# A seventh-product form for one more sequence unit, and two more gate/up units prepared inside the first FFN quarter

## The chip, the cores and the metric

The kernel runs on one core of a Trainium2 chip. The metric is the device time of one execution in microseconds, the median of three runs. Beside it stands one profiled execution with its trace.

The core has engines with queues of their own: TensorE (PE, with its weight loads as PEld), VectorE (DVE), ScalarE (ACT), GpSimd (POOL) and SyncE (SP). Each works through its own instructions in program order, so an instruction that waits holds back all that stands behind it on its engine. SP issues nearly all the DMAs.

## The reference

```python
a = einsum("bsd,ed->bse", x, dft_hid_re);  b = einsum("bsd,ed->bse", x, dft_hid_im)   # x after layer norm
y = einsum("ts,bse->bte", dft_seq_re, a) - einsum("ts,bse->bte", dft_seq_im, b)
h = A_x + y
gate, up = layernorm(h) @ w_gate, layernorm(h) @ w_up
out = h + (gelu(gate) * up) @ w_down
```

The sequence has 2048 rows, the model 448 features, the feed-forward part 1792. All is float32 outside; inside, each operand is split into a high and a low float16 part, and a product is three matmul terms (high by high, low by high, high by low).

## The kernel before

**DFT stage (0 to 347.7 us).** 16 row tiles of x are normalised and multiplied with the hidden DFT (feature tiles, matmuls at L457). The sequence DFT has 8 passes over the output rows; in each, 8 sequence units `u` (two row tiles each) are summed in PSUM (matmuls at L574). A unit is "plain" or an "S" unit. A plain unit is 24 matmuls of 448 columns. An S unit (listed in `S_UNITS`, 3 to 7 here) multiplies blocks as seven products of sums of blocks instead of eight, the Strassen scheme, in 42 matmuls of 224 columns. It pays for that with sums: in each pass VectorE forms `wsum` from the raw transform block `wr` (L518, L520, L522), ScalarE its high part and VectorE its low part (`wss`), and both form high and low of the raw blocks that are used alone (`ws`). The two feature tiles of an S unit need sums of `b` once.

**The planner.** A function `arranged()` gets every DFT piece of work as a task with an engine, a cost, a due time (shifted by kind through the table `SHIFT`) and what must come before it. It simulates the engines and writes the instructions in the order that it finds. Gate/up weights are prepared there too: raw weights are loaded, four sums are formed, high and low parts are made piece by piece (`gu_p`) and stored to DRAM (`w_dram`), from where a finished unit is loaded later as one tile `gw`.

**FFN stage (347.7 us to the end).** It has four quarters of 256 rows. In each, 14 gate/up units run one after the other; `t` counts them, 0 to 55. A unit has three PSUM banks X, Y, Z and seven products (matmuls at L1199, weights from `gw`); ScalarE does the gelu, VectorE and GpSimd the combinations into `hh`. In quarter 0 (t = 0 to 13) TensorE does nothing else; from t = 14 on, 21 matmuls of the down projection (`acc_d`, L1144) are woven into each unit. The down weights `wd` come in seven chunks: loaded (L230), summed on GpSimd, split by ScalarE and VectorE in a 448-column and a 1120-column part.

The order of TensorE in quarter 0 is written out by hand. At unit t: `x_close(t)` 5 matmuls, `x_open(t+1)` 6, `y_mid(t)` 6, `z_open(t+1)` 6, `y_open(t+1)` 6, `y_close(t)` 5, `z_close(t)` 5. So unit t+1 starts while unit t is being finished.

**Late units.** The units in `LATE` are not prepared in the DFT stage but in quarter 0, by `Weights.beat(k)` (L683), two beats to a unit: beat 2t stands after `y_mid(t)`, beat 2t+1 at the end of unit t. `late_prep` (L1421) starts unit f at beat `LATE[f]` and runs k = 0 to 5: sums in k = 0 and 1, one high part in each of k = 1 to 4, one low part in each of k = 2 to 5. The four parts are two of the raw weights (512 and 256 columns, from `gu_raw`) and two of the sums (512 each, from `gu_s`). The finished tile is stored at unit f for the later quarters (L698). Before the change, units 4, 8 and 12 are late.

## Time and profile before

| | |
|---|---|
| median of three runs | 706.2 us (705.64 to 706.41) |
| profiled execution, span of all instructions | 703.5 us |
| TensorE busy | 697.0 us |
| VectorE busy | 563.2 us |
| ScalarE busy | 408.0 us |
| GpSimd busy | 198.8 us |
| DMA moved | 139.74 MB |

The profiled execution's own time is given by its span, from the first to the last instruction; the median of the runs is 2.7 us above it. In the lines of a profile a number after a line label is the engine, the operation, what it writes and reads by the names of the program, the shape and the count; then the busy time and the mean of one in ns, then the idle time just before. In a timeline the first number is the start from the beginning of the span, the second the duration.

### The profile page before, as it was taken

What the parts mean: (1) busy time and instruction counts of PE and PEld (TensorE: products, weight loads), DVE (VectorE), ACT (ScalarE), POOL (GpSimd) and SP (SyncE); (2) the same over time, 40 slices, a digit from 0 to 9 for tenths busy, and PEclk for the clock granted to TensorE, in tenths of its full rate; (3) what the DMA queues carried; (4) which work ended last, traced back from release to release, by engine and by line L of the source; (5) the groups of instructions that cost most, each with busy time, mean ns of one, the idle gap of its engine ahead of it and who ended that gap; (6) DMA issues with size and microseconds to landing.
All of it is one profiled execution on the core that took longest, in us unless ns stands there. A gap on an engine that the chain in (4) does not pass through costs nothing.

```text
span 703.5 us, 15378 instructions
## 1 busy us (share of the span) xinstructions
PE 697.0 (99%) x6046; PEld 584.1 (83%) x6046; DVE 563.2 (80%) x1170; ACT 408.0 (58%) x862; POOL 198.8 (28%) x225
## 2 busy tenths in 40 slices
PE   8999999999999999999999999999999999999998
PEld 5556578878787878778888889999999999999998
DVE  6999999999999897989578877575765755786786
ACT  5776674667576565656267765555555544455432
POOL 0000000000000000001136754474664745647342
PEclk9999999999999999999999999999999999999999
DMA  9554555687988867777579665658466594545401
GB/s 330 160 128 114 142 170 184 233 245 227 228 275 202 283 177 261 262 253 281 182 258 353 204 211 170 191 180 199 170 195 190 178 200 173 181 158 166 151 27 54
DMA packets 81849, 139.74 MB, mean 199 GB/s; under 512 B 41712, under 2 KB 59376, under 8 KB 81776
## 3 DMA queue, kind: packets, MB, share of 16 engines
q1 hardware_dynamic: 81776, 138.76, 63.5%
q8 instruction: 47, 0.77, 0.5%
q14 instruction: 26, 0.21, 0.1%
HBM read 109.25 MB, written 20.19 MB: 184 GB/s over the span
## 4 chain that ended last, share of the span: by engine, by line
PE 95%; DMA 1%; ACT 1%; DVE 1%; issue 1%; SPq 0%; ACTq 0%; DVEq 0%
PE acc L574 38%; PE acc_d L1144 15%; PE pY L1199 14%; PE pZ L1199 9%; PE pX L1199 9%; PE ab L457 9%; DMA x<-in_x_dram 1%; DVE dn_w L110 0%; ACT dn_w L106 0%; SPq L429 0%; ACT xn_h L254 0%; DVE st_x L354 0%; DVE hh L1209 0%; ACT wd L106 0%; ACT g L1252 0%
## 5 line engine op out<-in xcount | busy, mean ns | idle before, releaser
L1199 PEld LDWEIGHTS <-gw 128*128 128x128 f16 x2184 | 213.1, 98 | 23.7 <-issue 1.0
L574 PE MATMUL acc<-b,ws 128*128 128x224 f16 (+1 forms) x1296 | 204.6, 301 | 0.0
L574 PEld LDWEIGHTS <-ws 128*128 128x128 f16 x1296 | 125.6, 98 | 53.2
L1199 PE MATMUL pY<-hops,gw 128*128 128x256 f16 x952 | 129.1, 273 | 0.0
L1144 PE MATMUL acc_d<-wd,dn_w 128*128 128x224 f16 x1050 | 122.3, 259 | 0.0
L574 PE MATMUL acc<-b,wss 128*128 128x224 f16 x960 | 118.2, 259 | 0.0
L235 POOL TENSOR_TENSOR wd_s<-wd 128x448 f32<-128x448 f32 x7 | 10.1, 1442 | 346.8 <-DMA wr<-in_w_seq_dram 330.0
L1144 PEld LDWEIGHTS <-dn_w 128*128 128x128 f16 x1050 | 101.1, 98 | 2.9
L574 PEld LDWEIGHTS <-wss 128*128 128x128 f16 x960 | 92.3, 98 | 0.1
L106 ACT ACTIVATE ws<-wr 128x256 f16<-128x256 f32 (+2 forms) x104 | 62.4, 637 | 41.1 <-PE acc L574 16.1
L1199 PE MATMUL pZ<-hops,gw 128*128 128x256 f16 x616 | 85.5, 273 | 0.4 <-DVE hh L1209 0.3
L1276 POOL TENSOR_TENSOR hh<-hh,c 128x256 f32<-128x256 f32 x56 | 46.3, 828 | 139.7 <-ACT c L1274 139.5
L1199 PE MATMUL pX<-hops,gw 128*128 128x256 f16 x616 | 83.3, 273 | 0.0
L112 DVE SCALAR_TENSOR_TENSOR ws<-wr,ws 128x256 f16<-128x256 f32 (+2 forms) x104 | 70.6, 709 | 1.4 <-ACT ws L106 1.3
L110 DVE TENSOR_TENSOR dn_w<-hh,dn_w 128x256 f16<-128x256 f32 x50 | 25.3, 506 | 53.1 <-ACT dn_w L106 52.8
L106 ACT ACTIVATE wss<-wsum 128x1024 f16<-128x1024 f32 x40 | 42.1, 1053 | 36.8 <-DVE wsum L522 21.1
L457 PEld LDWEIGHTS <-xT 128*128 128x128 f16 x352 | 33.9, 98 | 32.8 <-ACT xT L420 1.5
L110 DVE TENSOR_TENSOR dn_w<-dn_s,dn_w 128x640 f16<-128x640 f32 x50 | 54.6, 1092 | 7.4 <-ACT dn_w L106 6.7
L1243 ACT ACTIVATE u<-pY 128x256 f32<-128x256 f32 x56 | 21.4, 382 | 61.4 <-PE pY L1199 61.3
L1291 POOL TENSOR_TENSOR dn_s<-hh 128x256 f32<-128x256 f32 x42 | 52.8, 1258 | 0.0
L112 DVE SCALAR_TENSOR_TENSOR wss<-wsum,wss 128x1024 f16<-128x1024 f32 x40 | 48.8, 1220 | 4.1 <-ACT wss L106 4.0
L1238 ACT ACTIVATE pY<-pX 128x256 f32<-128x256 f32 x56 | 20.6, 368 | 50.3 <-PE pX L1199 50.3
...
## 6 DMA issues: line engine op xcount, KB each, us to landing
...
```

The source lines that it names most:

```text
L106: A.activation(dst, src, AF.Copy, scale=scale)
L110: V.tensor_sub(dst, src, hi)
L112: V.scalar_tensor_tensor(dst, src, scale, hi, op0=ALU.mult, op1=ALU.subtract)
L235: G.tensor_sub(s[:, 2:4], t[:, 0:2], t[:, 2:4])
L457: PE.matmul(feat[i][r][:, :D], xT[i][:, kx, :], w[:, kw, r * D : (r + 1) * D], start=n == 0, stop=n == 10,)
L574: PE.matmul(banks[k][:, cols], lhs, rhs, start=k not in begun, stop=stop, skip_group_check=True)
L1144: PE.matmul(acc[k // 2][:, k % 2 * HD : (k % 2 + 1) * HD], a_of(la, a), b_of(lb, b), start=first and m == 0 and k % 2 == 0, stop=last and ...
L1199: PE.matmul(ps, w[:, wl, wa + ws, :], ops[:, m + ms, :], start=first and n == 0, stop=last and n == len(terms) - 1, skip_group_check=True,)
L1238: A.activation(self.Y, self.X, AF.Copy)
L1243: A.activation(self.u2, self.Y, AF.Copy, scale=SC)
L1276: G.tensor_mul(c22, c22, self.c12)
L1291: E.tensor_sub(s[:, 2:4], t[:, 1:4:2], t[:, 0:4:2])
```

## The change

- Unit 2 becomes an S unit: `S_UNITS` is (2, 3, 4, 5, 6, 7). The raw parts of every S unit are made in one instruction of 768 columns where there were two of 256 and 512.
- In the DFT stage the statistics of the x tiles of units 7 and 4 go from VectorE to ScalarE, and two small steps of the reciprocal square roots too. The sums, splits and transposes of one normalised block of h (block (1,1), pass 3) go from the DFT stage to t = 0 to 4 of the FFN.
- `LATE` is {4: 1, 6: 6, 9: 11, 11: 16, 13: 21}: five late units instead of three, in five beats each instead of six. There are two raw buffers, and the next late unit's raw load is issued at k = 0 of the one before. The store is issued one beat after the last.
- Down's chunks are loaded from t = 4 on and prepared at t = 6 to 19; before they stood at t = 0 to 15. The preparation of the h blocks (2,0), (2,1) is spread differently over t = 14 to 27.
- The tables `SHIFT` and `HOLD` of the planner have other numbers, and the order of units in a pass is another.

```diff
-    S_UNITS, ... = (3, 4, 5, 6, 7), 3, 3, 2, 2
+    S_UNITS, ... = (2, 3, 4, 5, 6, 7), 3, 3, 2, 2
+    BY_SCALAR = (7, 4)
...
         if is_s(u):
-            return [(w[0], slice(0, 1), r[:, 0:1]), (w[0], slice(1, 3), r[:, 2:4])]
+            return [(w[0], slice(0, 3), r[:, 1:4])]
...
-            self.raw = pool.tile([P, 2, 6, P], F32, tag="raw", name=f"gu_raw{f}")
+            self.raw = pool.tile([P, 2, 6, P], F32, tag="raw", bufs=bufs, name=f"gu_raw{f}")
...
         def beat(self, k):
...
-            if k > 1:
-                s0, s1, src = parts[k - 2]
+            for n in ((), (), (0, 1), (2,), (3,))[k]:
+                s0, s1, src = parts[n]
                 lo_part(self.slots(1, s0, s1, src), src, self.slots(0, s0, s1, src), W_SC)
-            if 0 < k < 5:
-                s0, s1, src = parts[k - 1]
+            for n in ((), (0, 1), (2,), (3,), ())[k]:
+                s0, s1, src = parts[n]
                 hi_part(self.slots(0, s0, s1, src), src, W_SC)
...
-    LATE = {4: 0, 8: 7, 12: 15}
+    LATE = {4: 1, 6: 6, 9: 11, 11: 16, 13: 21}
...
+    WD0 = 6
+
+    def down_mid(t):
+        n, odd = divmod(t - WD0, 2)
+        if odd and 0 <= n < NC:
+            down_hi(n, 1)
+            if n + 1 < NC:
+                down_load(n + 1)
+        elif 0 < n < NC:
+            down_sums(n)
...
     def late_prep(beat):
-        if beat not in late_beats:
-            return
-        f, k = late_beats[beat]
-        gu[f].beat(k)
-        after = [v for v in LATE if v > f]
-        if k == 3 and after:
-            gu_late(after[0])
-        if k == 5:
-            gw[f] = gu[f].w
+        for f, k in late_beats.pop(beat, ()):
+            gu[f].beat(k)
+            after = [v for v in LATE if v > f]
+            if k == 0 and after:
+                gu_late(after[0])
+            if k == 1:
+                gw[f] = gu[f].w
+            if k == 4:
+                at(late_stores, beat + 1, f)
+        for f in late_stores.pop(beat, ()):
+            gu[f].store()
...
             cur.y_mid()
             late_prep(2 * t)
-            if t in LATE:
-                gu[t].store()
-            if t > 0 and t % 2 == 0 and t < 2 * NC:
-                down_hi(t // 2 - 1, 1)
+            do(t, 1)
+            down_mid(t)
             nxt.z_open()
             nxt.y_open()
             cur.y_close()
             cur.z_close()
             dn_ahead(t)
-            if t > 0:
-                down_prep(t - 1)
+            do(t, 2)
+            down_prep(t - WD0)
             late_prep(2 * t + 1)
+            do(t, 4)
```

Three places in the order of the instructions carry the numbers of the prediction.

The first is VectorE around the last late unit. Before, unit 12 was the last, and its low parts (`gw12` written from `gu_raw12` and `gu_s12`) stood among the work of units 8 to 10:

```order
L1209 SCALAR_TENSOR_TENSOR c12_8_5179<-pZ_8_5087,u2_8_5100 128x256
L112 SCALAR_TENSOR_TENSOR wd_4572<-wd_s_3_5054,wd_4572 128x1120
L112 SCALAR_TENSOR_TENSOR gw12_5149<-gu_raw12_4957,gw12_5149 128x512
L1209 SCALAR_TENSOR_TENSOR hh0_4599<-pZ_9_5153,u3_9_5216 128x256
L112 SCALAR_TENSOR_TENSOR gw12_5149<-gu_raw12_4957,gw12_5149 128x256
L1266 SCALAR_TENSOR_TENSOR hh0_4599<-pY_9_5134,g1_9_5197 128x256
L1209 SCALAR_TENSOR_TENSOR c12_9_5247<-pZ_9_5153,u2_9_5166 128x256
L112 SCALAR_TENSOR_TENSOR wd_4572<-wd32_4_5052,wd_4572 128x448
L112 SCALAR_TENSOR_TENSOR gw12_5149<-gu_s12_5117,gw12_5149 128x512
```

Now unit 13 is the last; its low parts stand among the work of units 11 and 12 (c12_11 is the last combination of unit 11, hh0 from pZ_12 follows the middle of unit 12, the pieces of `dn_w` are operands of the down projection):

```order
L1264 SCALAR_TENSOR_TENSOR c12_11_5458<-pZ_11_5359,u2_11_5372 128x256
L1347 TENSOR_TENSOR dn_s1_5460<-hh0_4652 128x128
L114 SCALAR_TENSOR_TENSOR wd_4625<-wd_s_2_5355,wd_4625 128x1120
L114 SCALAR_TENSOR_TENSOR gw13_5426<-gu_raw13_5218,gw13_5426 128x512
L114 SCALAR_TENSOR_TENSOR gw13_5426<-gu_raw13_5218,gw13_5426 128x256
L1264 SCALAR_TENSOR_TENSOR hh0_4652<-pZ_12_5432,u3_12_5494 128x256
L114 SCALAR_TENSOR_TENSOR gw13_5426<-gu_s13_5393,gw13_5426 128x512
L1321 SCALAR_TENSOR_TENSOR hh0_4652<-pY_12_5411,g1_12_5475 128x256
L1264 SCALAR_TENSOR_TENSOR c12_12_5529<-pZ_12_5432,u2_12_5445 128x256
L112 TENSOR_TENSOR dn_w0_5531<-hh0_4652,dn_w0_5531 128x256
L112 TENSOR_TENSOR dn_w0_5531<-dn_s0_5387,dn_w0_5531 128x640
L114 SCALAR_TENSOR_TENSOR wd_4625<-wd32_3_5430,wd_4625 128x448
```

Behind the last of these rows stands the fourth low part of `gw13`. On TensorE unit 13 opens (X) inside unit 12, with these rows; the third weight load is the first that reads a low part:

```order
L1254 MATMUL pX_12_5404<-hops0_167,gw12_5186 128x256
L1254 LDWEIGHTS gw13_5426 [waits Activation_49]
L1254 MATMUL pX_13_5477<-hops0_167,gw13_5426 128x256
L1254 LDWEIGHTS gw13_5426
L1254 MATMUL pX_13_5477<-hops0_167,gw13_5426 128x256
L1254 LDWEIGHTS gw13_5426 [waits DVE_49]
```

So the distance between the last late unit's low parts and their first use went from two units to less than one.

The second place is the last down chunk (6), on VectorE. Before, its 1120-column low part stood in unit 15, five units ahead of its first use at t = 20:

```order
L1266 SCALAR_TENSOR_TENSOR hh1_5516<-pY_15_5574,g1_15_5617 128x256
L1209 SCALAR_TENSOR_TENSOR c12_15_5684<-pZ_15_5619,u2_15_5603 128x256
L112 SCALAR_TENSOR_TENSOR wd_4572<-wd_s_6_5449,wd_4572 128x1120
```

Now it stands at the end of unit 19 (and its high part on ScalarE behind u2_20):

```order
L1321 SCALAR_TENSOR_TENSOR hh1_5605<-pY_19_6038,g1_19_6079 128x256
L1264 SCALAR_TENSOR_TENSOR c12_19_6144<-pZ_19_6081,u2_19_6062 128x256
L114 SCALAR_TENSOR_TENSOR wd_4625<-wd_s_6_6064,wd_4625 128x1120
L282 TENSOR_TENSOR tt_2_0_6159<-xn_h2_0_5667 128x256
```

It moved by four units, to just ahead of the matmuls of t = 20 that read it.

The third place is the store of the last late unit. SP's queue now has it here, between the loads of units 15 and 16 and that of chunk 4:

```order
L734 DMA w_dram11_164<-gw11_5258 128x3584
L247 DMA wd32_3_5430<-in_w_down_dram 128x896
L1121 DMA gw15_5468<-w_dram1_154 128x3584
L1121 DMA gw16_5539<-w_dram2_155 128x3584
L734 DMA w_dram13_166<-gw13_5426 128x3584
L247 DMA wd32_4_5570<-in_w_down_dram 128x896
```

On VectorE the first write of quarter 1's `hh1` (its pool takes over the space of `gw13` and the raw weights) stands behind these rows, and it waits for a DMA:

```order
L112 TENSOR_TENSOR dn_w1_5616<-hh0_4652,dn_w1_5616 128x256 [waits Activation_49]
L112 TENSOR_TENSOR dn_w1_5616<-dn_s1_5460,dn_w1_5616 128x640 [waits DVE_49,Activation_49]
L1264 SCALAR_TENSOR_TENSOR hh1_5605<-pZ_14_5572,u3_14_5639 128x256 [waits DMAHW5_49,DMAHW3_49,DMAHW6_49,DVE_49,Activation_49]
L1347 TENSOR_TENSOR dn_s2_5642<-hh0_4652 128x128
```

The semaphore DMAHW5 is the one that the store of `gw13` signals; before, the last late store was that of `gw12`, two units earlier.

More of the change, by code (lines that the diff above doesn't have):

```diff
@@ L128, in act_moments, with half_of @@
         A.activation(junk, src, AF.Square, bias=mv[:, 0:1], accum_out=mv[:, 1:2])
+    def half_of(mv, tag, pool=small, of=1):
+        n = mv.shape[1]
+        r = pool.tile([P, 4, n], F32, tag=f"r{n}" if pool is small else f"r_{tag}", name=f"r_{tag}")
+        A.activation(r[:, 1], mv[:, :, 1], AF.Identity, scale=-0.5 / (of * X_SC**2), bias=half_eps)
+        return r
     def root(mv, tag, of=1):
@@ L328 @@
     xt, xs, xT, norm_x = {}, {}, {}, {}
+    by_scalar = tuple((2 * u, 2 * u + 1) for u in BY_SCALAR)
+    junk = p1.tile([P, D], F16, name="junk")
     x_pairs = x.rearrange("(u g p) d -> u p g d", g=2, p=P)
@@ L356, in x_stats, with x_moments, x_of @@
             V.bn_aggr(mv[:, g, :], st)
+    def x_moments(i, tiles):
+        if i == tiles[0]:
+            norm_x[tiles] = small.tile([P, 2, 2], F32, tag="mv2", name=f"mv_x{i}")
+        act_moments(norm_x[tiles][:, tiles.index(i), :], xt[i][0], junk)
+    def x_of(tiles):
+        return D if tiles in by_scalar else 1
     def x_root(*tiles):
-        norm_x[tiles] = norm_x[tiles], root(norm_x[tiles], f"x{tiles[0]}")
+        mv, of, tag = norm_x[tiles], x_of(tiles), f"x{tiles[0]}"
+        r = half_of(mv, tag, small, of) if of > 1 else None
+        norm_x[tiles] = mv, root(mv, tag, of), r
     def x_rstd_steps(*tiles):
-        mv, sd = norm_x.pop(tiles)
+        mv, sd, r = norm_x.pop(tiles)
         found = []
-        steps = rstd_steps(found, mv, sd, f"x{tiles[0]}")
+        steps = rstd_steps(found, mv, sd, f"x{tiles[0]}", of=x_of(tiles), r=r)
         next(steps)
@@ L703 @@
     for k, u in enumerate(ORDER):
-        slots += [("F", i) for i in tiles_of[k]]
-        due = [v for v in ready if not is_s(v) or ORDER.index(v) < k - 1]
-        if k:
-            slots += [("U", 0, v) for v in due[:1]]
-            ready = [v for v in ready if v not in due[:1]]
+        for i in tiles_of[k]:
+            slots.append(("F", i))
+            if i % 2 == HALF.get(k, 1):
+                due = [v for v in ready if ORDER.index(v) < k - (2 if is_s(v) else BEHIND)]
+                slots += [("U", 0, v) for v in due[:1]]
+                ready = [v for v in ready if v not in due[:1]]
         ready.append(u)
@@ L714 @@
     mixed = plain[:]
-    for n, s in zip((1, 3, 4, 5, 7), S_UNITS):
+    for n, s in zip((1, 2, 3, 5, 6, 7), S_UNITS):
         mixed.insert(n, s)
@@ L763, in chain @@
         for k, cost in enumerate(costs):
-            last = [add(engine, cost, due, lambda k=k: step(k == 0), after=last, kind=kind)]
+            on, cost = cost if isinstance(cost, tuple) else (engine, cost)
+            last = [add(on, cost, due, lambda k=k: step(k == 0), after=last, kind=kind)]
         return last[0]
@@ L834 @@
         room = [steps[where["U", *units[g - WS_BUFS]]]] if g >= WS_BUFS else []
-        size = 0.9 if is_s(u) else 1.0
-        high = add("A", size, T[n] - 1.6 if g else -20.0, lambda p=p, u=u: seq_high(p, u), begin=-4.0, after=[load] + room, kind="whigh" if g else None)
-        low = add("V", 1.02 if is_s(u) else 1.16, T[n] - 0.4 if g else -20.0, lambda p=p, u=u: seq_low(p, u), after=[high], kind="wlow" if g else None)
+        size = 0.82 if is_s(u) else 1.0
+        high = add("A", size, T[n] - 1.6 if g else -20.0, lambda p=p, u=u: seq_high(p, u), begin=-4.0, after=[load] + room, kind="whigh" if g else "whigh0")
+        low = add("V", 0.87 if is_s(u) else 1.16, T[n] - 0.4 if g else -20.0, lambda p=p, u=u: seq_low(p, u), after=[high], kind="wlow" if g else "wlow0")
         done_with[g] = [low]
@@ L850 @@
     at_end = T[len(slots)]
+    IN_FFN = 3
     h_done, rooms, last_e = {}, {}, []
@@ L867 @@
         m = [add("A", 1.75, t0 + 9.0 + 4 * g, lambda q=q, j=j, g=g, p=p: ffn_moments(q, j, hp[q, j], g, junk_of(e_of[p])), after=[mixed_in], kind="mom") for g in range(2)]
[L868 to L869 removed]
+        t = add("A", 0.45, t0 + 14.0, lambda q=q, j=j: ffn_root(q, j), after=m, kind="hroot")
+        t = chain("V", RSTD, t0 + 15.0, lambda q=q, j=j: ffn_rstd_steps(q, j), [t], kind="hrstd")
         last_e, h_done[p] = m, [store, t]
@@ L1051 @@
             seq_mm(p, u, u == mine[0], u == mine[-1])
-        if t == p1_end:
-            first.close()
+    first.close()
     right.close()
@@ L1325, in dn_drain @@
     def dn_drain(p):
-        v = [ftile(f"v{k}", 1, f"v{k}_{p}", D) for k in range(2)]
+        v = fpool.tile([P, 2, D], F32, tag="v", name=f"v_{p}")
+        v = [v[:, k] for k in range(2)]
         return Drain(hr[p], acc_d[p], v, 1.0 / (H_SC * W_SC))
@@ L1451 @@
         d = t - NF
-        if d >= 0 and d % NC == 1:
+        if d >= 0 and d % NC == (4 if d // NC == 1 else 1):
             hr_load(d // NC)
@@ L1556 @@
     part_store(7, 1, 1)
-    assert not side
+    assert not side and not late_beats and not late_stores
 def _tiles(inputs):
```

157 lines of the change are left out of this document (107 added, 50 removed).

## The prediction

> **What bounds the kernel now.** I read the page's span and busy times first, then TensorE's waits, then the busy time by stage, and last the timeline of quarter 0. Busy times:
>
> ```profile
> span 703.5 us, 15378 instructions
> PE 697.0 (99%) x6046; PEld 584.1 (83%) x6046; DVE 563.2 (80%) x1170; ACT 408.0 (58%) x862; POOL 198.8 (28%) x225
> ```
>
> TensorE is busy for all but 6.5 us. Of its waits in the body of the program one alone is listed, the last row here; then the stretches of the DFT stage (from 99.4 us on) and of quarter 0: start to end, PE, PEld, DVE, ACT, POOL busy, granted clock, DMA share, GB/s:
>
> ```profile
> PE pZ L1199 <- DVE hh L1209: 0.3, 1, 0.3
> ...
> 99.40:347.70 248.30, 248.30 (x2102) 202.11 (x2101) 224.76 (x445) 153.52 (x291) 4.77 (x3) 1.00 0.76 237
> 348.00:411.00 63.00, 62.98 (x579) 56.30 (x577) 49.48 (x89) 43.62 (x104) 33.54 (x34) 1.00 0.72 253
> ```
>
> In both stretches TensorE has no gap, at a granted clock of 1.00. So less TensorE work shortens the span one for one, as long as nothing makes it wait; and every wait that appears is paid in full. VectorE is the next engine: 224.8 of 248.3 us in the DFT, 49.5 of 63.0 in quarter 0.
>
> **The gain.** A plain and an S unit on TensorE, as the chain of waits shows them:
>
> ```profile
> 27.77 4.54 PE acc L574 x24
> 61.82 4.03 PE acc L574 x42
> ```
>
> Unit 2 saves 0.51 us in each of 8 passes: −4.1 us. All the rest of the change puts no work on TensorE and takes none away, so this is the most that it can bring.
>
> **What the S unit costs VectorE in the DFT.** The durations by shape:
>
> ```profile
> L518 DVE TENSOR_TENSOR wsum<-wr 128x512 f32<-128x512 f32 x40 | 28.4, 709 | 9.0 <-DMA wr<-in_w_seq_dram 8.8
> L520 DVE TENSOR_TENSOR wsum<-wsum,wr 128x256 f32<-128x256 f32 x40 | 16.8, 419 | 0.3
> ...
> L112 DVE SCALAR_TENSOR_TENSOR wss<-wsum,wss 128x1024 f16<-128x1024 f32 x40 | 48.8, 1220 | 4.1 <-ACT wss L106 4.0
> ...
> L112 DVE SCALAR_TENSOR_TENSOR ws<-wr,ws 128x1024 f16<-128x1024 f32 x24 | 29.7, 1238 | 1.0 <-ACT ws L106 0.9
> L112 DVE SCALAR_TENSOR_TENSOR ws<-wr,ws 128x512 f16<-128x512 f32 x40 | 27.3, 684 | 0.1
> ...
> L110 DVE TENSOR_TENSOR b<-b,b 128x1568 f16<-128x1568 f32 x10 | 17.9, 1787 | 0.2 <-ACT b L106 0.2
> ...
> 0.00:348.00 348.00, 28.00 (x44) 24.01 (x44) 1.00 0.71 219
> ```
>
> Sums 0.71 + 2 × 0.42, their low part 1.22, raw low part of 768 columns 0.96 (between 0.684 and 1.238) in place of 1.24: +2.5 us a pass, +20 in all. The merged raw part saves about 0.14 in the 40 other S units, −5.6. The sums of the two feature tiles cost about +4. Two gate/up units fewer give back the low parts, 28.0 / 11 × 2 = −5.1 (the last row: VectorE and ScalarE time of `gu_p` for 11 units), and their sums, about −4. The x statistics, the small root steps and the block (1,1) give back some 3, 3 and 4. Together about −1 us, while TensorE's time shrinks by 4.1. VectorE's slack of 23.5 us in this stretch becomes about 20. ScalarE, at 153.5 of 248.3, has room for its share. The planner meets the due times by a simulation that I can't check from the trace; the bounds for waits at S units are 0 and the whole 4.1. I take +0.5, since the slack hardly shrinks.
>
> **What the late units cost in quarter 0.** This is where I expect the change to lose. VectorE's load there rises by two units' parts and sums and by the block (1,1), from 49.5 to about 58 of 63 us; the mean would still fit, but the order in which it stands does not. I walked the timeline of two steady units for the distances (start, duration):
>
> ```profile
> 401.37 0.51 DVE L1292 TENSOR_TENSOR dn_s<-hh 128x128 f32<-128x128 f32 x1
> 401.80 1.14 DVE L112 SCALAR_TENSOR_TENSOR wd<-wd,wd 128x448 f16<-128x448 f32 x1
> 401.95 0.82 PE L1199 MATMUL pY<-hops,gw 128*128 128x256 f16 x6
> 402.61 0.82 PE L1199 MATMUL pZ<-hops,gw 128*128 128x256 f16 x6
> 403.29 0.42 DVE L1209 SCALAR_TENSOR_TENSOR hh<-pZ,u 128x256 f32<-128x256 f32 x1 [0.34 <-ACT u L1257]
> 404.46 0.71 PE L1199 MATMUL pZ<-hops,gw 128*128 128x256 f16 x5
> 405.01 1.36 PE L1199 MATMUL pX<-hops,gw 128*128 128x256 f16 x11
> 405.28 0.42 DVE L1209 SCALAR_TENSOR_TENSOR c<-pZ,u 128x256 f32<-128x256 f32 x1 [0.19 <-PE pZ L1199]
> 405.62 0.41 DVE L110 TENSOR_TENSOR dn_w<-hh,dn_w 128x256 f16<-128x256 f32 x1
> 405.95 0.82 DVE L110 TENSOR_TENSOR dn_w<-dn_s,dn_w 128x640 f16<-128x640 f32 x1
> 406.21 0.82 PE L1199 MATMUL pY<-hops,gw 128*128 128x256 f16 x6
> 406.69 1.32 DVE L112 SCALAR_TENSOR_TENSOR wd<-wd_s,wd 128x1120 f16<-128x1120 f32 x1
> ```
>
> One matmul of 256 columns takes 0.109 us in a row (11 from 405.01 to 406.21). Independent instructions of VectorE start some 0.07 us before the former one's end. The low parts of late units in quarter 0:
>
> ```profile
> L112 DVE SCALAR_TENSOR_TENSOR gw<-gu_raw,gw x6: 420/684/1023, 356.8 to 390.9; 128x512 f16<-128x512 f32 x3, 128x256 f16<-128x256 f32 x3
> ...
> L112 DVE SCALAR_TENSOR_TENSOR gw<-gu_s,gw x6: 680/784/1209, 361.0 to 395.3; 128x512 f16<-128x512 f32 x6
> ```
>
> Unit 13 is the last late unit, and its low parts come one beat too late. Let s be the start of a `z_close`; the combination `c` begins at s + 0.82 (404.46 to 405.28).
>
> (a) `x_open(13)`: behind c12_11 stand dn_s (0.35), the 1120-column part of `wd` (0.43 later, then 1.25), and the first low part of gw13 (0.68): ready at s + 0.82 + 0.35 + 0.43 + 1.25 + 0.68 + 0.1 = s + 3.6. TensorE wants it at the third weight load, s + 0.55 + 7 × 0.109 = s + 1.3. Wait 2.3 us.
>
> (b) `z_open(13)`: the third low part stands behind hh of unit 12, which starts 1.34 after `y_mid` (401.95 to 403.29): 1.34 + 0.35 + 0.78 + 0.1 = 2.6. Wanted at 0.66 + 0.22 = 0.9. Wait 1.7.
>
> (c) `y_mid(13)`: the fourth low part stands behind c12_12, two parts of dn_w (0.34, then 0.75) and a 448-column part of `wd` (1.06): s + 0.82 + 0.34 + 0.34 + 0.75 + 1.06 + 0.78 + 0.1 = s + 4.2. Wanted at s + 1.75 + 0.22 = s + 2.0. Wait 2.2.
>
> (d) `z_open(11)`: the third low part of gw11 stands behind c12_9 and the 1120-column part: s + 0.82 + 0.35 + 1.25 + 0.78 + 0.1 = s + 3.3, wanted at s + 0.55 + 1.20 + 0.66 + 0.22 = s + 2.6. Wait 0.7.
>
> Units 4, 6 and 9 start their beats at least as many ahead as 11 and have no `wd` parts or fewer in front: 0. Before, unit 12's last low part was ready two units early, which is why the trace shows no such wait. While TensorE waits, VectorE's `hh`, `c` and `dn_w` of the running unit wait with it, so it doesn't catch up for the next: I add the four. Bounds: with the shortest parts (0.42 and 0.68) and the dn_w parts early, 5.9 together; with VectorE late by its higher load, and low parts of 1.0 to 1.2, 9.0. I take 6.9.
>
> The low part takes 0.68 us at its shortest here and 1.2 at its longest, with GpSimd busy for 33.5 of 63.0 us of this quarter; the walk uses the medians. [...]
>
> **The last down chunk.** In quarter 1 the order on TensorE is `y_open`, `x_close`, `z_open`, first 8 down matmuls:
>
> ```profile
> 414.23 0.82 PE L1199 MATMUL pY<-hops,gw 128*128 128x256 f16 x6
> 414.88 0.71 PE L1199 MATMUL pX<-hops,gw 128*128 128x256 f16 x5
> ...
> 415.69 0.36 ACT L1243 ACTIVATE u<-pY 128x256 f32<-128x256 f32 x1
> 415.95 1.12 ACT L106 ACTIVATE wd<-wd_s 128x1120 f16<-128x1120 f32 x1
> 416.08 0.93 PE L1144 MATMUL acc_d<-wd,dn_w 128*128 128x224 f16 x8
> ```
>
> (e) Chunk 6 now has its high part behind u2_20 and its low part behind that, and the down matmuls of t = 20 read it. From the start of `y_open(20)`: 0.82 + 0.1 + 0.36 + 1.12 + 0.1 + 1.25 = 3.75; the second down matmul is wanted at 1.85 + 0.1. Wait 1.8 (1.5 to 2.2). Chunks 3 to 5 at t = 15, 17, 19 put a 1120-column part in front of the unit's own `u`, `c` and `dn_w` steps; (g) 0.5 for that, 0 to 1.0.
>
> **The store.** (f) hh of quarter 1 takes gw13's space, so its first write, at t = 14, waits until the store has landed. That store takes, from issue to landing (shortest, median, longest):
>
> ```profile
> DMA to landing us min/median/max: 8.0/8.6/9.2
> ...
> 409.27 0.71 PE L1199 MATMUL pX<-hops,gw 128*128 128x256 f16 x5
> ...
> 413.40 0.71 PE L1199 MATMUL pZ<-hops,gw 128*128 128x256 f16 x5
> ```
>
> It is issued when the fourth low part is there, which is (c)'s moment. `z_close(14)` overwrites the Z that hh reads; from (c) to it TensorE has the rest of unit 13 and most of unit 14, about 7.05 us (`y_mid` at 406.21 to the unit's end at 409.27 is 3.1, less two matmuls 2.9; unit 14 from there to its `z_close` at 413.40 is 4.1). 8.6 + 0.4 for hh − 7.05 = 2.0 of wait. Bounds 2.7 (9.2 to landing) and 0 (a store under less traffic; it would have to land in 6.6).
>
> Other edits at nothing: the prep of (1,1) at t = 0 to 4 and the split of (2,0), (2,1) at t = 14 to 27 are hidden by VectorE's free time, 13.5 of 63.0 us in quarter 0 before, and TensorE reads their results a unit or more later. The loads of down are issued a unit ahead of their sums on GpSimd, and these a unit ahead of their split; GpSimd, busy for 33.5 of 63.0, waits there for no one that TensorE needs in quarter 0. If that cover were gone, each would show as a wait of about one low part, 0.8.
>
> **Sum.** Span 703.5 − 4.1 + 0.5 + 6.9 + 1.8 + 0.5 + 2.0 = 711.1. With 2.7 for what lies between span and median, 713.8; I put it at 713.4, since a wait for anything between (c) and `z_close(14)` shortens (f) by as much. Ends, from the median 706.2: all low −4.1 + 5.9 + 1.5 = +3.3, 709.5; all high −4.1 + 2.0 + 9.0 + 2.2 + 1.0 + 2.7 = +12.8, 719.0, which would need every term at its end at once.
>
> **Rivals.**
> (B) Only (a) to (c) and (e) are real, at their low ends, and the store lands early: −4.1 + 0.5 + 2.0 + 1.5 + 1.8 + 1.5 = +3.2, 709.4. For it speaks that (a) to (c) delay TensorE, and so give VectorE time to clear what is not tied to the running unit; against it, that (d), (e) and (f) lie in other units. Chance 0.17.
> (C) The low parts are on time and only the gain is left: 702.1. VectorE's mean load, 58 of 63, speaks for it. Against it speaks the order: the low part stands behind c12_11, whose input comes from TensorE itself as `z_close(11)` ends, so VectorE's free time earlier in the quarter doesn't help. It would need c12_11, dn_s, the part of `wd` and the low part, 3.0 us in a row by the walk, to be done in 0.7. Faster from the point at which (a) to (g) come to less than 3.6 in all. Chance 0.09, with 0.03 more for no change.
> (D) VectorE is late in the DFT too: unit 2 now needs 1.5 + 1.2 + 1.0 us of VectorE within the 4.03 of a unit; waits of 0.5 in each pass take the gain back: 713.4 + 3.6 = 717.0. For it, 224.8 of 248.3 busy and another order of the planner; against, that VectorE's work falls. Chance 0.11.
> Forecast A: 0.60.
>
> **Numbers.** 713.4 us. The range 707.0 to 717.5 takes in B and leaves C, no change and the upper half of D outside. A measurement of this kernel can tell 0.2%, 1.4 us, from no change: faster 0.09 (C), same 0.03, slower 0.88 (A, B, D).
>
> **What would show it.** TensorE's waits should list `gw` L114 from VectorE at L1254, three or four times, 0.7 to 2.3 us, between t = 10 and 13; one `acc_d` from `wd` of 1.8 at t = 20; one pZ from hh of 2 us at t = 14, with a DMA behind hh. The DFT stage should end near 344 us. Wrong would be: TensorE without a gap in quarter 0 (then C), or its waits inside the DFT (then D).

## The result, and the profile after

The changed kernel takes 721.84 us in the median of four runs (721.52 to 723.91), against 705.92 us before: 1.0229 times the time, with an interval of 1.021 to 1.0247. It is slower, as forecast, but by 15.9 us where 7 were forecast, and beyond the top of the range (717.5). The profiled execution is the longest of the four, 2.1 us above the median, so the stretches below add up to 18.6 us of span. Two executions in a slow state (1219 us of e6_nosums, 1227 us of the kernel before) are left out of all times below.

The page of the changed kernel, span and busy times:

```profile
span 722.1 us, 15609 instructions
PE 698.0 (97%) x6190; PEld 598.2 (83%) x6190; DVE 585.8 (81%) x1140; ACT 421.0 (58%) x870; POOL 200.0 (28%) x226
```

TensorE's busy time did not fall by 4.1 us, although its work did: part of it ran at a lower clock (0.57 from 387 to 389.5 us); the rest of the difference I have not taken apart. The gain is seen better in where the first gate/up matmul starts, 345.95 us against 347.5 before. TensorE's waits, first of the DFT stage from 60 us on, then of quarter 0 (347 to 424 us), then the largest of quarter 1 (424 to 520 us):

```profile
PE acc L610 <- DVE wss L114: 0.9, 2, 0.5
PE acc L610 <- DVE ws L114: 0.4, 1, 0.4
PE ab L489 <- DMA xT<-xs: 0.2, 1, 0.2
...
PE pZ L1254 <- DVE gw L114: 3.0, 2, 2.3
PE pX L1254 <- DVE gw L114: 2.8, 1, 2.8
PE pZ L1254 <- DVE hh L1264: 2.3, 3, 1.6
PE pY L1254 <- ACT pY L1293: 2.0, 1, 2.0
PE pY L1254 <- DVE gw L114: 1.9, 1, 1.9
PE pX L1254 <- DMA gw<-w_dram: 0.5, 1, 0.5
...
PE pZ L1254 <- DVE hh L1264: 2.0, 5, 0.5
PE acc_d L1191 <- DVE wd L114: 1.1, 1, 1.1
PE acc_d L1191 <- ACT wd L108: 0.3, 1, 0.3
```

Before, the same three stretches had one wait of 0.3 us. The forecast waits are there, at the forecast places. These rows of TensorE's timeline are (d), (a), (b) and (c) in that order, the four rows on `gw`:

```profile
400.21 0.61 PE L1254 MATMUL pZ<-hops,gw 128*128 128x256 f16 x4 [0.65 <-DVE gw L114]
...
411.03 0.61 PE L1254 MATMUL pX<-hops,gw 128*128 128x256 f16 x4 [2.77 <-DVE gw L114]
...
414.86 0.61 PE L1254 MATMUL pZ<-hops,gw 128*128 128x256 f16 x4 [2.34 <-DVE gw L114]
...
420.54 0.61 PE L1254 MATMUL pY<-hops,gw 128*128 128x256 f16 x4 [1.91 <-DVE gw L114]
```

What the forecast did not have stands at 376 to 389 us, in units 7 and 8. First SP's queue, then what ScalarE, VectorE and TensorE did:

```profile
365.83 7.13 SPq L332 DMA_TRANSPOSE hops<-xs  x2
373.06 0.53 SPq L1121 DMA_DIRECT2D gw<-w_dram  x1
373.69 2.52 SPq L332 DMA_TRANSPOSE hops<-xs  x2
376.26 0.59 SPq L247 DMA_DIRECT2D wd<-in_w_down_dram  x1
...
381.56 0.58 ACT L108 ACTIVATE wd<-wd 128x448 f16<-128x448 f32 x1 [4.17 <-DMA wd<-in_w_down_dram]
382.17 1.31 DVE L114 SCALAR_TENSOR_TENSOR wd<-wd,wd 128x448 f16<-128x448 f32 x1 [3.58 <-ACT wd L108]
383.25 1.36 PE L1254 MATMUL pY<-hops,gw 128*128 128x256 f16 x11 [1.99 <-ACT pY L1293]
386.21 1.23 PE L1254 MATMUL pZ<-hops,gw 128*128 128x256 f16 x5 [1.60 <-DVE hh L1264]
387.23 2.31 PE L1254 MATMUL pX<-hops,gw 128*128 128x256 f16 x11
```

The four transposes of block (1,1), moved into quarter 0, hold SP's queue from 365.8 to 376.2 us. The load of down's chunk 0 stands behind them, is issued at 376.26 and is there at 381.5. ScalarE stands at its split for 4.2 us, VectorE behind it for 3.6, and the running unit's `pY` and `hh` behind them; TensorE loses 2.0 and 1.6 us, and then runs 11 matmuls in 2.31 us that take 1.36 elsewhere. The granted clock of these stretches:

```profile
385.00:387.00 2.00, 0.79 (x4) 0.56 (x4) 2.00 (x5) 1.41 (x2) 2.00 (x3) 0.69 1.07 448
387.00:389.50 2.50, 2.50 (x16) 1.83 (x14) 2.25 (x4) 0.38 (x1) 0.55 (x1) 0.57 0.83 259
```

### The profile page after: what moved, and what is told of

It reads as the page before. It is cut to its first block, busy times and chain, and to the rows that moved or that the text cites. A ratio compares the mean times of both kernels' runs of the same rounds, so it can differ in the third digit from the quotient of the medians.

```text
span 722.1 us, 15609 instructions
## 1 busy us (share of the span) xinstructions
PE 698.0 (97%) x6190; PEld 598.2 (83%) x6190; DVE 585.8 (81%) x1140; ACT 421.0 (58%) x870; POOL 200.0 (28%) x226
## 4 chain that ended last, share of the span: by engine, by line
PE 67%; DVE 20%; DMA 5%; ACT 3%; issue 3%; SPq 1%; DVEq 0%; ACTq 0%
PE acc L610 18%; PE acc_d L1191 14%; PE pY L1254 11%; PE ab L489 8%; PE pZ L1254 8%; PE pX L1254 8%; DVE ws L114 3%; DVE wss L114 3%; DVE wsum L554 2%; DMA wr<-in_w_seq_dram 2%; DVE dn_w L112 2%; DMA wd<-in_w_down_dram 1%; DVE wd L114 1%; DVE wsum L556 1%; DMA x<-in_x_dram 1%
## 5 line engine op out<-in xcount | busy, mean ns | idle before, releaser
L610 PE MATMUL acc<-b,ws 128*128 128x224 f16 (+1 forms) x1248 | 187.2, 288 | 0.4 <-DVE ws L114 0.4
L610 PEld LDWEIGHTS <-ws 128*128 128x128 f16 x1248 | 120.7, 98 | 36.3 <-DVE ws L114 0.7
L610 PE MATMUL acc<-b,wss 128*128 128x224 f16 x1152 | 142.1, 259 | 0.9 <-DVE wss L114 0.9
L610 PEld LDWEIGHTS <-wss 128*128 128x128 f16 x1152 | 110.8, 98 | 1.4 <-DVE wss L114 1.4
L108 ACT ACTIVATE wss<-wsum 128x1024 f16<-128x1024 f32 x48 | 50.6, 1055 | 58.6 <-DVE wsum L558 30.8
L108 ACT ACTIVATE ws<-wr 128x768 f16<-128x768 f32 (+1 forms) x64 | 56.7, 889 | 28.1 <-PE acc L610 15.2
L114 DVE SCALAR_TENSOR_TENSOR ws<-wr,ws 128x768 f16<-128x768 f32 (+1 forms) x64 | 64.9, 1017 | 0.0
L114 DVE SCALAR_TENSOR_TENSOR wss<-wsum,wss 128x1024 f16<-128x1024 f32 x48 | 58.6, 1220 | 6.7 <-ACT wss L108 6.5
L112 DVE TENSOR_TENSOR dn_w<-hh,dn_w 128x256 f16<-128x256 f32 x50 | 27.8, 556 | 42.1 <-ACT dn_w L108 41.8
L489 PE MATMUL ab<-wh_hi,xT 128*128 128x448 f16 x224 | 45.7, 353 | 1.7 <-ACT xT L452 0.9
```

The lines of the kernel that those rows point to most:

```text
L108: A.activation(dst, src, AF.Copy, scale=scale)
L112: V.tensor_sub(dst, src, hi)
L114: V.scalar_tensor_tensor(dst, src, scale, hi, op0=ALU.mult, op1=ALU.subtract)
L489: PE.matmul(feat[i][r][:, :D], xT[i][:, kx, :], w[:, kw, r * D : (r + 1) * D], start=n == 0, stop=n == 10,)
L610: PE.matmul(banks[k][:, cols], lhs, rhs, start=k not in begun, stop=stop, skip_group_check=True)
```

## The experiments

All times are medians. The runs were taken in five groups (e1 to e5, e6 to e9, e10 to e13, e14 and e15, e16 and e17), with the kernel before beside each; it took 705.4 to 706.4 us there, so less than a microsecond between runs of different groups means nothing. "Waits in quarter 0" are gaps in TensorE's timeline there, from one start to the next against the usual step; where matmuls at a lower clock are in the sum, the text says so.

| run | what is different from the changed kernel | us |
|---|---|---|
| (before) | | 705.9 |
| (changed) | | 721.8 |
| e1_beat | late units 9, 11, 13 one beat earlier | 716.7 |
| e2_load | chunk 0 loaded ahead of the transposes | 720.2 |
| e3_both | late units 1, 2, 3 beats earlier, and that load | 713.7 |
| e5_plain2 | unit 2 plain again | 736.3 |
| e6_nosums | e3, no sums on GpSimd | 710.0 |
| e7_actlow | e3, ten low parts off VectorE | 713.4 |
| e8_three | three late units, and that load | 722.3 |
| e9_front | work of quarter 0 brought forward | 719.3 |
| e10_block | block (1,1) back in the DFT stage | 718.5 |
| e11_block_rep | e3 and e10 | 712.4 |
| e12_two | e2, late units 1 or 2 beats earlier, one more buffer for the chunks | 714.9 |
| e13_all | block (1,1) back, buffers, chunks 2 units earlier | 711.9 |
| e14_actlow | e13, ten low parts off VectorE | 712.0 |
| e15_nosums | e13, no sums on GpSimd | 707.4 |
| e16_vsums | e13, these sums on VectorE | 709.5 |
| e17_memset3 | e13, GpSimd fills in place of sums | 708.3 |

### The two causes named so far, taken away singly and together

e1_beat:

```diff
-    LATE = {4: 1, 6: 6, 9: 11, 11: 16, 13: 21}
+    LATE = {4: 1, 6: 6, 9: 10, 11: 15, 13: 20}
```

> The changed kernel with the last three late units started one beat earlier: LATE 9 at 10, 11 at 15, 13 at 20; nothing else. Theory (the low parts stand too late in VectorE's order): the waits on gw of 2.9 (x_open 13), 2.1 (y_mid 13) and 0.8 (z_open 11) go, that of z_open(13) falls from 2.5 to about 0.8, as its part now stands at the end of unit 11 behind a 1120-column part of wd: 721.8 - 7.5 = 714.3 us. Rival (VectorE has too much to do in quarter 0 as a whole): the waits come back elsewhere, less than 3 us saved, above 718.8.

Measured 716.7, a gain of 5.1: between the two. The waits on `gw` went from 7.7 us to one of 2.1 (at `z_open(13)`, more than the 0.8 expected), but waits of TensorE on `hh` grew from 2.3 to 3.5.

e2_load:

```diff
-        (4, 4, lambda: down_load(0)),
+        (2, 4, lambda: down_load(0)),
```

> The changed kernel with the load of down chunk 0 issued at the end of t = 2 in place of t = 4, that is ahead of the four DMA transposes of block (1,1) in SP's queue. Theory (the transposes hold SP's queue for 10 us, the load lands late, ScalarE and VectorE stand behind it, and TensorE waits): the waits of 0.7, 2.2 and 1.8 us between 379 and 387 us go, and the half clock behind them (1.4 us): 721.8 - 6 = 715.8 us. Rival (the prep of (1,1) makes VectorE late there, not the load): no change, 721 to 722.

Measured 720.2, a gain of only 1.6. The mechanism was right and the price was not. The first split of chunk 0 on ScalarE no longer waits:

```profile
376.97 0.57 ACT L108 ACTIVATE wd<-wd 128x448 f16<-128x448 f32 x1
```

But GpSimd's first sum still waits, for 6.7 us, until the block's transposes have landed, since its tile takes the space of the block's split operand; ScalarE's second split waits 1.6 us for the sums. TensorE waits for VectorE at other places instead (quarter 0):

```profile
PE pZ L1254 <- DVE gw L114: 3.1, 2, 1.7
PE pX L1254 <- DVE gw L114: 2.8, 1, 2.8
PE pZ L1254 <- DVE hh L1264: 2.4, 4, 0.9
PE pY L1254 <- DVE gw L114: 1.9, 1, 1.9
```

The low clock moved too: it is gone at 387 us (1.00 from 381.5 to 390 us), and here it follows the gaps on `gw` (0.60 from 407 to 415.5 us), at a price of some 2 us.

e3_both:

```diff
+    LATE = {4: 1, 6: 6, 9: 10, 11: 14, 13: 18}
...
+        (2, 4, lambda: down_load(0)),
```

> Both repairs, with LATE 9 at 10, 11 at 14, 13 at 18. If the two causes are separate and their prices add: 721.8 - 8.3 (all four waits on gw) - 6 = 707.5 us. Rival (VectorE's sum of work in quarter 0 is the bound): the waits move, above 711.

Measured 713.7: a gain of 8.1, not 14. The rows on `gw` are gone, but TensorE waits for `hh` instead (4 times, 3.9 us), and VectorE has no time left in two stretches of quarter 0 (VectorE busy, then clock, DMA share, GB/s):

```profile
390.00:398.50 8.50, 8.43 (x12) 1.00 0.60 205
398.50:407.00 8.50, 8.45 (x14) 1.00 0.66 231
```

So the waits on low parts and the late load were two of the places at which VectorE's lateness surfaced. With both gone it surfaces at the next one.

### What fills VectorE: work, or GpSimd beside it

e6_nosums, on top of e3:

```diff
-        G.tensor_sub(s[:, 2:4], t[:, 0:2], t[:, 2:4])
-        t22 = t.rearrange("p (a b) d -> p a b d", a=2)
-        G.tensor_add(s[:, 0:2], t22[:, :, 0], t22[:, :, 1])
-        G.tensor_add(s[:, 4], t[:, 0], t[:, 3])
+        G.memset(s, 0.0)
```

> Both repairs (as before: LATE 9 at 10, 11 at 14, 13 at 18, the load of chunk 0 at t = 2), and GpSimd's three sums of each down chunk left out: one fill of the same tile with zeros stands for them, so five of the seven parts of the down weights are zero and the output is not the reference's. VectorE's instructions are the same as with both repairs alone. There VectorE was busy for 8.4 of 8.5 us in the stretches from 390 to 407 us, and the 512-column low parts from gu_s took 1.24 us each against 0.68 in the DFT. Theory 1 (GpSimd's sums slow VectorE's two-input instructions): these low parts fall to about 0.7 us, and the 6.0 us of waits in quarter 0 to about 2: 713.7 - 4 = 709.7. Theory 2 (it is the amount of VectorE's work alone): durations and waits stay, 713 to 714.

e7_actlow, on top of e3:

```diff
+                if n > 1:
+                    hi_part(self.slots(1, s0, s1, src), src, W_SC)
+                    continue
                 lo_part(self.slots(1, s0, s1, src), src, self.slots(0, s0, s1, src), W_SC)
```

> Both repairs, and the low parts of the late units' sums not computed: ScalarE writes a copy of the high part there, so the output is not the reference's. It takes 10 instructions of 512 columns off VectorE (0.7 to 1.6 us each, 7.4 us of them between 378 and 406) and puts 6.2 us on ScalarE. If VectorE's amount of work in the second half of quarter 0 is the bound, the 6.0 us of waits there go nearly all: 713.7 - 5.5 = 708.2. If ScalarE or the order is, they stay: 713 or more.

Without GpSimd's sums 710.0, 3.7 us less, with VectorE's list of instructions unchanged. With ten instructions fewer on VectorE 713.4, 0.3 less: a miss. There the waits on `hh` fell to 0.9, but one of 2.1 us on ScalarE's `pY` came, behind chunk 1: its load is issued only when chunk 0 has left the one buffer, and landed 7 us later. The low parts from `gu_s` between 378 and 406 us, with both repairs, and with the sums taken away besides:

```profile
L114 DVE SCALAR_TENSOR_TENSOR gw<-gu_s,gw 128x512 f16<-128x512 f32 x6 | 7.4, 1240 | 0.0
```

```profile
L114 DVE SCALAR_TENSOR_TENSOR gw<-gu_s,gw 128x512 f16<-128x512 f32 x6 | 4.4, 736 | 0.0
```

The same instruction takes 1240 ns in the mean in this stretch with GpSimd's sums and 736 without. In the DFT stage, where GpSimd does next to nothing (4.8 of 248 us), it takes 726; the row is of the kernel before:

```profile
L112 DVE SCALAR_TENSOR_TENSOR gu_p<-gu_s,gu_p 128x512 f16<-128x512 f32 x22 | 16.0, 726 | 0.0
```

This pair still mixes two things, since without sums nobody waits for them either; the last pair of runs parts them.

### Single parts undone

e5_plain2:

```diff
-    S_UNITS, ... = (2, 3, 4, 5, 6, 7), 3, 3, 2, 2
+    S_UNITS, ... = (3, 4, 5, 6, 7), 3, 3, 2, 2
...
-    for n, s in zip((1, 2, 3, 5, 6, 7), S_UNITS):
+    for n, s in zip((1, 3, 4, 5, 7), S_UNITS):
```

> The changed kernel with unit 2 as a plain unit again (and its place in a pass as before), all else as changed. TensorE has 8 x 0.51 = 4.1 us more to do. Theory: of the 2.2 us of waits that the DFT stage has after the change, most come from the S unit's sums on VectorE and go, so 721.8 + 4.1 - 2 = 724 us. Rival (the waits come from the planner's new order alone): they stay, 726.

Measured 736.3, 14.5 more, where 4.1 was the plain unit's own. The rest lies in the feature stage (12 to 101 us): gaps of 12.1 us in TensorE's timeline at feature tiles, slower matmuls behind two of them included (14 take 5.54 and 4.74 us there, 2.81 elsewhere). Behind it, from 101 us to the end of the DFT stage, TensorE does not wait at all, where the changed kernel has gaps of 1.8. That fits the theory, by which the waits of the later passes come with the S unit, but does not show it: the 12 us of gaps ahead also gave VectorE time. The planner's table belongs to its set of units, and this run can't price the unit alone.

e8_three:

```diff
-    LATE = {4: 1, 6: 6, 9: 11, 11: 16, 13: 21}
+    LATE = {4: 1, 8: 8, 12: 15}
```

> The changed kernel with three late units (4 at beat 1, 8 at 8, 12 at 15), so that two units' preparation goes back into the DFT stage, and the load of chunk 0 at t = 2. VectorE gets about 9 us more to do in the DFT stage, where it had 285 - 265 = 20 us free, and 9 us less in quarter 0. Theory (VectorE's work in quarter 0 and its order are the loss): the waits of quarter 0, 15 us, fall below 3; the DFT stage has the S unit's cost in full now, 2 to 8 us of waits: 711 to 715. Rival (the waits in quarter 0 come from the moved block (1,1) and down's chunks): they stay above 8, and 718 or more.

Measured 722.3, the rival's number but not its reason. The DFT stage pays 3.8 us in one wait on ScalarE (`acc` L595); the stores of the last prepared pieces hold SP for 7.5 us at the start of quarter 0, so that raw weights and `gw` come late; and before 400 us ScalarE waits 4.1 us for a down chunk. TensorE's waits from 100 to 440 us, the largest:

```profile
PE pZ L1254 <- DVE hh L1264: 4.5, 4, 3.3
PE acc L610 <- ACT acc L595: 3.8, 1, 3.8
PE pY L1254 <- ACT pY L1293: 3.1, 2, 2.6
```

Two late units fewer are no cure by themselves.

e9_front:

```diff
+    LATE = {4: 0, 6: 4, 9: 9, 11: 13, 13: 17}
...
+        (1, 4, lambda: down_load(0)),
+        (2, 4, lambda: ffn_transpose(1, 1, (0,))),
+        (3, 4, lambda: ffn_transpose(1, 1, (1,))),
+        (3, 4, lambda: ffn_transpose(1, 1, (2,))),
+        (4, 4, lambda: ffn_transpose(1, 1, (3,))),
+        (4, 4, lambda: down_sums(0)),
...
+    WD0 = 5
```

> A repair that moves VectorE's work of quarter 0 to its front, where it was busy for 5.3 and 6.1 of 8.5 us: LATE 4 at 0, 6 at 4, 9 at 9, 11 at 13, 13 at 17; block (1,1) prepared by the middle of t = 2 and its transposes at t = 2 to 4; chunk 0 loaded at t = 1; all chunks one unit earlier. If VectorE's work only stands too late, the waits of quarter 0 fall from 6.0 to 2 and that on chunk 6 (1.7 us) goes: 713.7 - 5.5 = 708. If its sum is too large for the quarter, 711 to 714. If the DMAs in front (raw loads, transposes) come late, 714 or more.

Measured 719.3, in the third case. GpSimd's first sum takes the space of the block's split operand, so it waits for the transposes to land; ScalarE's split waits for the sum, and TensorE for ScalarE:

```profile
382.77 1.14 ACT L108 ACTIVATE wd<-wd_s 128x1120 f16<-128x1120 f32 x1 [6.78 <-POOL wd_s L255]
```

e10_block, and e11_block_rep with the edits of e3 besides:

```diff
-    IN_FFN = 3
+    IN_FFN = -1
...
-        (0, 1, lambda: ffn_sums(1, 1, (0,))),
...
-        (4, 4, lambda: ffn_transpose(1, 1, (3,))),
```

> The changed kernel with the sums, splits and transposes of block (1,1) put back into the DFT stage, nothing else. It takes 4.2 us of VectorE, about 10 us of SP's queue and the wait for the transposes off quarter 0, and puts 4.2 us of VectorE into the end of pass 3 and pass 4 of the DFT. Theory (the block's transposes hold SP's queue and with it down's first load): the waits at 379 to 390 us, 6 us with the half clock, go, the DFT gains up to 2 of waits: 717 to 718. Rival (VectorE's sum alone counts): only some 2 us go, 720 or more.

> Block (1,1) back in the DFT stage, together with both repairs (LATE 9 at 10, 11 at 14, 13 at 18; chunk 0 loaded at t = 2). With VectorE no longer full from 381 to 407 us, the 6.0 us of waits in quarter 0 fall to about 2, the DFT takes up to 2 more: 713.7 - 4 + 1 = 710.7. If the DFT pays as much as quarter 0 gains: 713 to 714.

718.5 and 712.4: gains of 3.3 on the changed kernel and 1.3 on e3, so a little less than the theory each time. With the block alone put back, the chain at 376 to 389 us is gone (TensorE's waits on ScalarE and on the load of `gw`), and the four waits on `gw` stand as they were, at 2.8, 2.3, 1.9 and 0.7:

```profile
PE pZ L1254 <- DVE gw L114: 3.0, 2, 2.3
PE pX L1254 <- DVE gw L114: 2.8, 1, 2.8
PE pY L1254 <- DVE gw L114: 1.9, 1, 1.9
```

The block's move into quarter 0 saved the DFT stage nothing that stands out: the first gate/up matmul starts at 346.47 us here against 345.95, but at 345.1 and 344.7 in e11 and e13, which have the block back too, and between 344.8 and 346.0 in kernels with the DFT stage of the changed one (e1, e2, e3, e6, e7). The move cost 3.3 net.

### All repairs, and what is left

e12_two gives chunks 1 and 3 a buffer of their own, with one raw buffer for the space; e13_all adds the block's return and starts the chunks two units earlier:

```diff
-        wd32[n] = fpool.tile([P, 4, HD], F32, tag="v", name=f"wd32_{n}")
+        pool, tag = (scr, "wd_odd") if n in (1, 3) else (fpool, "v")
+        wd32[n] = pool.tile([P, 4, HD], F32, tag=tag, name=f"wd32_{n}")
...
+    LATE = {4: 0, 6: 5, 9: 9, 11: 14, 13: 19}
...
+    WD0 = 4
```

> Down's chunks 1 and 3 get a buffer of their own in quarter 0, so that chunks 1 to 4 are loaded two chunks ahead; for the space the late units' raw weights have one buffer (next load at k = 2), and LATE is 4 at 0, 6 at 5, 9 at 9, 11 at 14, 13 at 19. Block (1,1) stays in quarter 0. Theory (with one buffer a chunk's load is issued only when the chunk before is split, and lands 5 to 7 us later, while ScalarE and GpSimd stand waiting for it): ScalarE's waits for down's loads go, and with them some 3 us: 710 to 711. Rival (VectorE full, and slowed by GpSimd, is all there is): 713 or more.

> The buffers of the run before, block (1,1) back in the DFT stage, and all chunks two units earlier (first at t = 4), which also takes away the waits on chunk 6 (1.7 us) and most of those at t = 15 to 19 (1.8 us). If the causes named so far are all: DFT waits 2.5 to 4.5, quarter 0 about 2, quarter 1 about 1: 706 to 708. To beat the kernel before it would have to come under 704.5; I give that 0.15.

714.9 and 711.9. ScalarE's waits for the loads are gone in both, but the first did not gain on e3: the rival. In the second the waits on chunk 6 are gone too. In its quarter 0 6.8 us remain: 5.1 us of gaps, the largest ahead of matmuls that wait for VectorE's `hh` and `c`, and 1.7 us for matmuls at a granted clock of 0.51 behind the longest gap. One of its runs kept the full clock (1.00) and took 711.6, so the clock is not what keeps it slow. The next two runs took one thing more away each, by the edits of e7 and e6.

> The run with all repairs, and the low parts of the late units' sums replaced by copies on ScalarE (the output is not the reference's): 10 instructions, 7 to 9 us, off VectorE, 6.2 us onto ScalarE. If VectorE's amount of work is what is left, the 6.8 us of waits in quarter 0 fall below 1.5: 711.9 - 5.3 = 706.6, or less. If it is the order or ScalarE, they stay above 4: 709 or more.

> The run with all repairs, and GpSimd's sums of the down chunks replaced by one fill with zeros (five of seven parts of the down weights are zero, the output is not the reference's); VectorE's instructions are unchanged. If GpSimd's slowing of VectorE is a main part of what is left, the mean of the low parts from gu_s falls to 0.7 us, and 3 to 4 of the 6.8 us of waits go: 708 to 709. If the amount of work alone counts: 711 to 712.

712.0 and 707.4. Ten instructions off VectorE, and 6.4 us of its busy time with them, gained nothing. The sums off GpSimd took 4.5 us, with no instruction taken from VectorE. The amount of VectorE's work alone is therefore not what is left; my forecast for e14 was wrong. ScalarE, which has ten instructions more in e14, is not what took their place: all of TensorE's listed waits in quarter 0 are on VectorE's `hh` and `c` (4.3 us), though VectorE is busy for only 44.7 of 61 us. What makes `hh` late is what stands just ahead of it on VectorE. A sum of 256 columns takes 1.35 us beside one of GpSimd's there, and 0.42 in the mean in e15:

```profile
395.25 1.44 POOL L253 TENSOR_TENSOR wd_s<-wd 128x448 f32<-128x448 f32 x1
395.63 1.35 DVE L681 TENSOR_TENSOR gu_s<-gu_raw 128x256 f32<-128x256 f32 x1
...
396.90 0.41 DVE L1269 SCALAR_TENSOR_TENSOR hh<-pZ,u 128x256 f32<-128x256 f32 x1
...
397.36 0.71 PE L1259 MATMUL pZ<-hops,gw 128*128 128x256 f16 x5 [1.09 <-DVE hh L1269]
```

The last two runs part two causes of which neither had been shown by then: my guess that GpSimd's reading slows those instructions of VectorE beside it that have two inputs (the sharing of the expectations), and GpSimd being occupied:

```diff
-        G.tensor_sub(s[:, 2:4], t[:, 0:2], t[:, 2:4])
+        V.tensor_sub(s[:, 2:4], t[:, 0:2], t[:, 2:4])
...
```

(e16_vsums, all three sums so) and, for e17_memset3,

```diff
+        for _ in range(3):
+            G.memset(s, 0.0)
```

> The run with all repairs, with the three sums of a down chunk on VectorE in place of GpSimd: about 0.62 + 0.62 + 0.39 = 1.6 us a chunk more for VectorE, 5 to 6 us in quarter 0, and GpSimd's 3.4 us a chunk gone. If GpSimd slows VectorE by sharing, this is cheaper: 709 or less (711.9 before). If VectorE's amount of work is the bound after all, 714 or more.

> As the run without sums, but GpSimd fills the tile three times (3 x 1.03 us, about what the sums take, with no operand to read; five of seven parts of the down weights are zero, so the output is not the reference's). If it is the shared access of two-input instructions, VectorE runs as without sums: 707 to 708, low parts from gu_s at 0.7 us. If GpSimd's occupation (its multiplications of hh behind the sums, the splits waiting for them) costs the 4.5 us: 711 to 712.

709.5 and 708.3. In e17 GpSimd is occupied as long as with sums, yet the time is 0.9 us from that without them. The stretch from 347 to 408 us of e13, e15 and e17, with PE, PEld, DVE, ACT and POOL busy, then one group of low parts in it:

```profile
347.00:408.00 61.00, 57.09 (x499) 49.34 (x497) 51.10 (x89) 39.38 (x95) 29.38 (x30) 0.97 0.80 289
...
L114 DVE SCALAR_TENSOR_TENSOR gw<-gu_raw,gw 128x256 f16<-128x256 f32 x5 | 4.1, 812 | 0.0
```

```profile
347.00:408.00 61.00, 59.18 (x533) 51.93 (x532) 48.02 (x95) 43.37 (x103) 18.94 (x22) 1.00 0.83 303
...
L114 DVE SCALAR_TENSOR_TENSOR gw<-gu_raw,gw 128x256 f16<-128x256 f32 x5 | 3.1, 627 | 0.0
```

```profile
347.00:408.00 61.00, 58.54 (x529) 51.41 (x527) 47.25 (x95) 42.74 (x101) 29.50 (x31) 1.00 0.82 299
...
L114 DVE SCALAR_TENSOR_TENSOR gw<-gu_raw,gw 128x256 f16<-128x256 f32 x5 | 3.1, 629 | 0.0
```

The first and the third have GpSimd busy for the same 29.4 us. The low part takes 812 ns beside GpSimd's reading and 629 beside its filling, the same as without the sums. Not each shape is as clear (the 512-column part from `gu_raw` takes 928, 701 and 809), but as a whole VectorE does 95 instructions in 48.0 us without sums and 95 in 47.3 with the fills, where 89 took 51.1 beside the sums. So it is GpSimd's reading of operands that costs, and not the place in its queue. The instructions that it lengthens have both inputs in SBUF: the sums of 384 columns from `gu_s` and `gu_raw` take 866 ns in e13 and 652 in e15, though those from `gu_raw` alone take 555 and 653. `hh` and `c`, which read one input from PSUM, take 0.42 us in each of these runs. That the place of the inputs decides was not shown, since no run changes it alone. The three runs give the cost a size in this kernel: 3.6 to 4.5 us of 711.9, or 2.9 to 3.8 when each run is set against the kernel before beside it.

e16 shows the same from the other side: VectorE gets three instructions more for each chunk, its busy time from 347 to 408 us grows by only 0.8 us (51.85 for 51.10, with 105 instructions for 89), and the time falls by 2.4, or by 1.7 against the kernel before beside it. It is the fastest of the kernels that compute the whole, at 1.0048 times the time before (1.0033 to 1.0063). Nothing tried here beats the kernel before, and e15, which leaves the sums out, doesn't either. I ran no further version for that.

## Why the prediction was right or wrong

| step | forecast us | measured in the profiled execution |
|---|---|---|
| S unit on TensorE | −4.1 | about −4.0: 1.55 earlier at the first gate/up matmul, with 2.4 of new gaps ahead of it |
| waits in the DFT | +0.5 (0 to 4.1) | +2.4, 1.8 of it at S units (at 175 and 276 us) |
| (a) to (d), low parts of 13 and 11 | 2.3, 1.7, 2.2, 0.7 | 2.8, 2.3, 1.9, 0.7 |
| (e) chunk 6 at t = 20 | 1.8 | 1.4 in two waits, 1.9 with the restarts |
| (f) store of gw13 | 2.0 | 0: it landed in 4.4 us |
| (g) chunks at t = 15 to 19 | 0.5 | 1.8 |
| other edits | 0 | 6.0 at t = 6 to 8 with the clock of 0.57, 1.3 more on hh and the like in quarter 0, 0.8 at t = 27 |

**Right.** The direction, and the reason that the gain is bought with waits in quarter 0. The walk through VectorE's order gave each of the four waits on `gw` to within 0.6 us and their sum to within 0.8 (7.7 for 6.9), from rows of the trace before alone. They stood as they were when the chain ahead of them was taken away (e10), so it is no luck that they fit. Chunk 6 came out where and nearly as large as forecast.

**Wrong: "Other edits at nothing".** That step said that the loads of down are issued a unit ahead, and that GpSimd waits for no one that TensorE needs. Both halves failed at the same place. I had listed the four transposes with the block, but had not walked them through SP's queue, where they held 10.4 us, nor looked at what stands behind them there: the load of chunk 0, raw weights and a load of `gw`. Of the seven loads of chunks only that of chunk 0 was waited for, 4.2 us by ScalarE and 9.6 by GpSimd. Without the transposes (e10) it is issued 10 us earlier, at 366.2 us, and ScalarE does not wait for it: the queue failed, and not the distance in units. The one buffer, where there were two before, counts only in the faster versions (in e3 ScalarE waits 1.7 us for a chunk). At t = 6 to 8 that is 6 us of the 11 by which the profiled execution went past its forecast of 711.1; undone alone it gave back 1.6 (e2) or 3.3 (e10).

**Wrong: that waits add.** I added the four waits on the ground that VectorE does not catch up while TensorE waits. In this direction it held. But I took them for the loss itself, and the experiments show them to be places where lateness surfaces: taking them away gave back 5.1 of 7.5, the load 1.6 of 6, both 8.1 of 14. Behind them stands VectorE with no time left (8.4 of 8.5 us in e3), of which I had said that "the mean would still fit".

**Mis-sized: the slowing by GpSimd.** The walk took the four low parts on my list at the medians of before, 0.68 and 0.78 us; with all four at the 1.21 us of the longest row it would have been 1.8 more. But GpSimd's sums also lengthen other VectorE instructions with both inputs in SBUF, the sums of the late units among them (866 ns for 652 at 384 columns). Before, VectorE had 13.5 us free in quarter 0 to take that up; now it has hardly any where the sums stand. With all named causes removed it is 2.9 to 4.5 us.

**Mis-sized: VectorE's load in the DFT.** The sum gave about −1 us. From 99.4 to 345.9 us VectorE is busy for 229.6 us, against 224.8 before: +5. So its free time there shrank from 23.5 to 17 us and not to 20, and the term for the waits, 0.5, measured 2.4. The upper end of the sum used 2.0 for it where the working had named 4.1; with that the end would have been 721.1 and not 719.0.

**Too large: the store.** (f) used 8.6 us to landing, the median of three stores before. The five stores after took from 4.4 to 10.6, and the last was the fastest: it had landed at 425.0 us, 2.4 us before `hh` was written. The 0.2 us that TensorE waited for that `hh` stand behind VectorE's steps of `dn_w`. Why this store landed sooner was not tested.

**The rivals.** C (no waits) is refuted by the rows on `gw`; so is B (709.4), since (a) to (c) stand above its low ends and (d) is there. D, that the DFT stage gives the gain back, was half true in amount, 2.4 of 4.1, though not with 0.5 us in each pass. It is independent of the rest, and should have been a larger term of the sum and not a rival.

**Still open.** After e16, 5 us of waits in quarter 0 and 2 to 3 in quarter 1 are left; I have not tried to order VectorE's work there anew. What the S unit alone costs the DFT stage with a planner's table made for it is not measured either: the one with the unit taken away had the wrong table.
